# Hash attention with a token mixer: hash directions packed on the host and split in three operations, engine durations and delays of the order model read from the trace, and the order set anew

## The chip, the cores and the metric

The kernel runs on one core of a Trainium2 chip. The metric is the device time of one execution in microseconds; lower is better. The engines are TensorE (PE, with its weight loads as PEld), VectorE (DVE), ScalarE (ACT), GpSimd (POOL) and SyncE (SP), which issues the DMAs here.

## The reference

Two stages follow each other, for 4 batches, 8 heads, 768 tokens and 64 features a head:

```python
q_bits = (einsum('bhsd,dk->bhsk', q, proj) > 0)      # 6 hash bits of a query, k likewise
mask = q_bucket[:, :, :, None] == k_bucket[:, :, None, :]
scores = where(mask, q @ k.T / sqrt(D), -1e9)
attn = exp(scores - max(scores)); attn = attn / (sum(attn) + 1e-9)
x = (attn @ v), heads side by side                    # 4 x 768 x 512
theta = x @ w_theta
y = w_tok_r @ (x * cos(theta)) + w_tok_i @ (x * sin(theta))   # over the tokens
u = x + y
out = u + max(u @ w_ch, 0)
```

## The kernel before

All matrices of one batch stay on the chip. Heads go in pairs (16 pairs). The names below are those of the rows that the text shows.

**Attention.** `prep_qk` loads the transposed queries and keys of a pair (`nat`), splits each into a rounded part and its remainder (`hl`: the rounding on ACT, the subtraction, "split", on DVE or POOL), and multiplies by the hash directions (`pb`, the direction matmuls; `pst` holds the directions, positive and negated, in a rounded and a remainder part). The signs of `pb` become extra rows of the operands `qt`, `kt`, so that scores of another bucket come out hugely negative. `maxima` computes the scores once for the row maxima (`sq`, nine DVE maxima `mc` a head), transposes them (`pmx`) and puts the row back by DMA. `step` computes the scores again with the keys on the partitions (`st`), in nine chunks of 512 a head; ACT takes the exponential (`pf`). Then comes the product with the values (`po`) in one of two forms:

- the two-part form: ACT rounds `pf` to 16 bits (`p1`), POOL takes the remainder (`p2`), and three 16-bit matmuls are made per tile of 128 keys and 128 queries (two with 65 columns, one with 64), with the values in two 16-bit parts (`vv`);
- the full form, for the pairs listed in `FULL`: one fp32 matmul with 65 columns per tile, from `pf` and fp32 values (`vw`), and no `p1`, `p2`.

DVE scales the result into the batch's tile `x` (`recip`, `norm`).

**Mixer.** `moe`: each of 6 token tiles is transposed (`pt_x`), split (`h_x`, `l_x`) and multiplied by `w_theta` (`ps_th`); DVE and ACT reduce the angle, ACT takes cosine and sine for a group of tiles at once (a table load stands ahead of each group), DVE multiplies with `x` (`f`), ACT and POOL or DVE split the product (`z`, the angles' remainder); 216 matmuls `py` mix the tokens; a second product `ps_r` by `w_ch` ends it. The weights of the tokens are unpacked from 64-bit words during the first batch (`prep_wtok`, tile `wst`: low and high word on DVE, sign and magnitude on ACT, product on POOL or DVE, split into `wtk`).

**The order.** Every piece of work is an `op` with a priority, the engines that may do it with a duration for each, the ops that it needs and the buffers that it holds. `issue_all` runs a list schedule over them at build time: an engine that is free takes the ready op of the lowest key, and the instructions are issued in the order so found. The durations and the delays between engines in it (`SAME`, `LAT` and the numbers in the op calls) decide the order alone; on the chip, an instruction starts when the one ahead of it on its engine and the semaphores that it waits for allow. Where PE has nothing to do in the model during the first 190 us, a filler matmul is issued (`fill<-idle`), which nothing uses. Priorities come from the constants at the end of the file (for example `W0`, the place of the token weights among the steps).

Of the kernel before, what the change touches and what calls it, by code (L numbers as in the profile page):

```python
# [32 lines left out]
def lsh_attention_moe_kernel(ctx: ExitStack, tc: tile.TileContext, qk, wt, v, proj, w_theta, w_ch, aff, out):  # L33
# [4 lines left out]
    NB = proj.shape[1]  # L38
    DM = w_theta.shape[0]
    P = 128  # L40
# [19 lines left out]
    affs = const.tile([P, 2], F32, name="affs")  # L60
# [10 lines left out]
    pp = const.tile([P, NB], F32, name="pp")  # L71
    pst = {}
    for nm in "qk":
        for part in "hl":
            pst[nm, part] = const.tile([P, P], F32R, name=f"pst_{nm}{part}")
            DVE.memset(pst[nm, part].bitcast(F32), 0.0)
# [6 lines left out]
    SAME = {"PE": 0, "ACT": 120, "DVE": 115, "POOL": 160}  # L83
# [30 lines left out]
    def issue_all():  # L114
# [98 lines left out]
        while todo:  # L213
            progress = False
            for e in START:
# [34 lines left out]
                lat = LAT.get(e, 0)  # L250
# [20 lines left out]
                if TRACE is not None:  # L271
                    TRACE.append((e, o.name, o.phase, now, dur))
                tick += 1
                same = [c for c in succ[o] if e != "SP" and list(c.alts) == [e]]
                o.same = same
                heapq.heappush(events, (now + dur + lat, tick, o))
                heapq.heappush(events, (now + dur, -tick, []))
                if same:
                    heapq.heappush(events, (now + dur + SAME[e], tick + 0.5, same))
                for c in succ[o]:  # L280
                    c.unissued -= 1
                    c.at = max(c.at, now + dur + (SAME[e] if c in same else lat))
# [10 lines left out]
            while events and events[0][0] <= now:  # L293
# [3 lines left out]
                else:  # L297
# [4 lines left out]
                    nexts = [c for c in succ[o] if c not in o.same]  # L302
# [31 lines left out]
    def load_consts():  # L334
        for j in range(2):
            dma(pp[j * D : (j + 1) * D, :], proj)
        dma(affs, aff)

    def split_proj():
        for nm, base, first in (("q", 0, 1.0), ("k", 32, -1.0)):  # L340
            for j in range(2):
                rows = slice(j * D, (j + 1) * D)
                for n, sgn in enumerate((first, -first)):
                    c0 = base + j * 2 * NB + n * NB
                    h_, l_ = (pst[nm, part][rows, c0 : c0 + NB] for part in "hl")
                    DVE.tensor_scalar(h_, pp[rows, :], sgn, None, ALU.mult)
                    DVE.scalar_tensor_tensor(l_, pp[rows, :], sgn, h_.bitcast(F32), ALU.mult, ALU.subtract)

    cload = op("consts", QKL + 0.03, on("SP", [(625, 0)] * 3, load_consts))
    proj_ready = op("pst", QK0, on("DVE", 2200, split_proj), [cload])  # L350


# [71 lines left out]
    def prep_wtok(n, prio):  # L424
# [22 lines left out]
        def split():  # L447
# [11 lines left out]
            "POOL": (100 + 1650, lambda: POOL.tensor_tensor(t["f"], t["f"], t["sg"], ALU.mult)),  # L459
            "DVE": (60 + 830, lambda: DVE.tensor_tensor(t["f"], t["f"], t["sg"], ALU.mult)),  # L460
        }, [d, e], sl)
        i = op("wth", prio, on("ACT", 100 + 640, lambda: ACT.activation(hi16, t["f"], AF.Copy, scale=wsc[:, col])), [g, h_], sl)
        wready["tk"].append(op("wtl", prio, on("DVE", 60 + 830, split), [i], sl))
        wst_last.append(wready["tk"][-1])

    def join_wtok(prio):
# [25 lines left out]
        o = op("vall", prio, on("DVE", 130, row), [o], [sa])  # L492
        o = op("vall", prio, on("PE", 130, everywhere), [o], [sa])
# [8 lines left out]
    def prep_v(b, hp, prio):  # L502
# [104 lines left out]
        d = op("vmean", prio, on("PE", 220, mean), [c], [svb, sm_])  # L607
        e = op("vclr", prio, on("POOL", 600, clear), [r], [sv])
# [623 lines left out]
```

## Time and profile before

| | |
|---|---|
| median of 3 runs | 859.31 us (858.04 to 859.6) |
| the profiled execution, its time | 857.55 us |
| its span, first to last instruction | 855.7 us |
| mean granted TensorE clock | 0.99 |
| PE busy | 819.1 us, of which filler matmuls 53.1 us (131) |
| DVE, ACT, POOL busy | 554.3, 514.9, 471.2 us |

Busy is the time in which an engine has an instruction in flight; PE's matmuls overlap, so a busy PE is not one at its peak. A row of the timeline gives start and length in us, engine, line, operation, tiles written and read, shapes, a count of merged instructions, and in brackets the idle time before and who ended it. The group rows give busy time and mean ns, then the idle time before them. The stages are the start (0 to 80 us), the rest of the first batch's attention (to some 220 us), then three times the attention of a batch beside the mixer of the batch before it, and the mixer of batch 3 alone (from some 760 us).

### The profile page before, as it was taken

What the parts mean: (1) busy time and instruction counts of PE and PEld (TensorE: products, weight loads), DVE (VectorE), ACT (ScalarE), POOL (GpSimd) and SP (SyncE); (2) the same over time, 40 slices, a digit from 0 to 9 for tenths busy, and PEclk for the clock granted to TensorE, in tenths of its full rate; (3) what the DMA queues carried; (4) which work ended last, traced back from release to release, by engine and by line L of the source; (5) the groups of instructions that cost most, each with busy time, mean ns of one, the idle gap of its engine ahead of it and who ended that gap; (6) DMA issues with size and microseconds to landing.
All of it is one profiled execution on the core that took longest, in us unless ns stands there. A gap on an engine that the chain in (4) does not pass through costs nothing.

```text
span 855.7 us, 17506 instructions
## 1 busy us (share of the span) xinstructions
PE 819.1 (96%) x6726; PEld 575.0 (67%) x6726; DVE 554.3 (65%) x957; ACT 514.9 (60%) x881; POOL 471.2 (55%) x503
## 2 busy tenths in 40 slices
PE   8998999999999999997999999999999999999997
PEld 3477678768666577765766767778667766676455
DVE  5876879985897755766788555565796445138123
ACT  3264877786984635684897545557987453559000
POOL 3332875685786525794569645576669463653100
PEclk9996999999999999999999999999999999999999
DMA  7375576534433332544331524334342412000001
GB/s 222 80 194 156 109 209 199 165 76 108 99 87 79 115 81 72 137 100 94 81 88 33 130 68 109 73 91 109 78 96 59 103 25 65 13 15 1 1 12 62
DMA packets 33779, 78.99 MB, mean 92 GB/s; under 512 B 6520, under 2 KB 10808, under 8 KB 33696
## 3 DMA queue, kind: packets, MB, share of 16 engines
q1 hardware_dynamic: 33696, 77.88, 36.4%
q8 instruction: 53, 0.87, 0.4%
q14 instruction: 30, 0.25, 0.1%
HBM read 32.51 MB, written 6.29 MB: 45 GB/s over the span
## 4 chain that ended last, share of the span: by engine, by line
PE 81%; DVE 7%; ACT 6%; issue 2%; POOL 2%; DMA 1%; SPq 0%; POOLq 0%; ACTq 0%; DVEq 0%
PE py L79 20%; PE st L79 13%; PE po L79 13%; PE ps_r L79 8%; PE ps_th L79 7%; PE sq L79 6%; PE fill L79 5%; PE pb L79 4%; DVE mc L767 2%; ACT pf L845 2%; PE pt_u L956 1%; DVE hl L645 1%; DVE mc L776 1%; ACT p L851 1%; PE pt_x L956 1%
## 5 line engine op out<-in xcount | busy, mean ns | idle before, releaser
L857 POOL TENSOR_TENSOR p<-pf,p 128x512 f16<-128x512 f32 x252 | 301.4, 1219 | 135.4 <-ACT p L851 87.8
L845 ACT ACTIVATE pf<-st 128x512 f32<-128x512 f32 x288 | 166.4, 593 | 123.9 <-PE st L79 99.4
L767 DVE TENSOR_REDUCE mc<-sq 128x1 f32<-128x512 f32 (+1 forms) x288 | 190.3, 683 | 63.1 <-PE sq L79 61.4
L79 PE MATMUL py<-z,wtk 128*128 128x512 f16 x864 | 213.1, 380 | 0.0
L79 PE MATMUL st<-qt,kt 108*128 108x512 f32 (+3 forms) x768 | 194.8, 367 | 3.7 <-ACT pf L845 3.1
L851 ACT ACTIVATE p<-pf 128x512 f16<-128x512 f32 x252 | 152.3, 630 | 30.1 <-PE po L79 27.9
L79 PEld LDWEIGHTS st<-qt,kt 108*128 108x128 f32 (+1 forms) x768 | 120.7, 192 | 27.2 <-ACT pf L845 13.2
L79 PEld LDWEIGHTS <-p 128*128 128x128 f16 x3024 | 113.0, 98 | 35.6 <-issue 20.7
L79 PE MATMUL po<-vv,p 128*128 128x65 f16 x3024 | 131.2, 194 | 3.4 <-POOL p L857 2.5
L79 PEld LDWEIGHTS <-wtk 128*128 128x128 f16 x864 | 73.5, 98 | 83.9 <-issue 16.3
L79 PE MATMUL sq<-kt,qt 108*128 108x256 f32 (+1 forms) x384 | 123.8, 390 | 1.1 <-DVE mc L767 0.6
L79 PEld LDWEIGHTS sq<-kt,qt 108*128 108x128 f32 x384 | 67.7, 192 | 22.5 <-DVE mc L767 8.0
L1045 POOL TENSOR_TENSOR z<-f,z 128x512 f16<-128x512 f32 x35 | 49.7, 1432 | 52.4 <-ACT z L1039 52.1
L79 PE MATMUL ps_r<-wch,h_u 128*128 128x512 f32 x192 | 62.4, 406 | 0.7 <-ACT h_u L961 0.7
L79 PE MATMUL ps_th<-wth,h_x 128*128 128x512 f32 x192 | 62.2, 405 | 0.9 <-ACT h_x L961 0.9
L79 PE MATMUL fill<-idle 128*128 128x512 f16 x131 | 53.1, 409 | 6.0 <-DVE idle L68 1.6
L961 ACT ACTIVATE h_u<-pt_u 128x512 fp32r<-128x512 f32 x24 | 14.2, 595 | 73.9 <-PE pt_u L956 73.9
L1080 DVE SCALAR_TENSOR_TENSOR x<-ps_r,x 128x512 f32<-128x512 f32 x24 | 16.6, 691 | 60.0 <-PE ps_r L79 60.0
L1034 DVE SCALAR_TENSOR_TENSOR f<-x,zr,z 128x512 f32<-128x512 f32 x48 | 50.1, 1079 | 4.5 <-POOL z L1045 2.1
L788 POOL TENSOR_SCALAR fl<-row 6x128 f16<-6x128 f32 x32 | 23.3, 729 | 38.9 <-DVE row L784 24.6
L79 PE MATMUL po<-vw,pf 128*128 128x65 f32 x288 | 39.1, 287 | 4.7 <-ACT pf L845 4.6
L552 POOL TENSOR_TENSOR vb<-vb 128x384 f32<-128x384 f32 x16 | 16.1, 1009 | 48.3 <-DVE vv L549 23.3
(146 smaller groups left out, 1110.5 us busy)
## 6 DMA issues: line engine op xcount, KB each, us to landing
nat<-in_qk_dram SPq DMA_DIRECT2D x32, 384.0 KB
qt<-hl SPq DMA_DIRECT2D x31, 384.0 KB
kt<-hl SPq DMA_DIRECT2D x31, 384.0 KB
wst<-in_wt_dram SPq DMA_DIRECT2D x12, 768.0 KB
vb<-in_v_dram SPq DMA_DIRECT2D x16, 384.0 KB
out_dram<-x SPq DMA_DIRECT2D x24, 256.0 KB
qt<-hl SPq DMA_DIRECT2D x62, 96.0 KB
kt<-hl SPq DMA_DIRECT2D x62, 96.0 KB
```

Source lines behind the costliest of these rows:

```text
L79: PE.matmul(out_, l, r, start=start, stop=stop, skip_group_check=True)
L552: POOL.tensor_tensor(t["vb"][:, :, 0:3], t["vb"][:, :, 0:3], t["vb"][:, :, 3:6], ALU.add)
L767: DVE.tensor_reduce(col()[:, cs], u["sq"], AX.X, ALU.max)
L788: POOL.tensor_scalar(t["fl"], t["row"].bitcast(F32), -BIG / 4, PSC, ALU.is_lt, ALU.mult)
L845: ACT.activation(wide("pf", spf, F32), u["st"], AF.Exp, scale=1.0 / math.sqrt(D))
L851: ACT.activation(o_, u["pf"], AF.Copy)
L857: return lambda: eng.tensor_tensor(wide("p2", sp2, F16), u["pf"], u["p1"], ALU.subtract)
L956: PE.transpose(u["pt"][:, c], src()[:, c * P : (c + 1) * P], ident)
L961: ACT.activation(u["hi"], u["pt"], AF.Copy)
L1034: DVE.scalar_tensor_tensor(u["f"], tl[b][:, tt], t["zr"][:, 2 * tt + r : 2 * tt + r + 1], t["zw"][r][:, tt], ALU.mult, ALU.mult)
L1045: return lambda: eng.tensor_tensor(t["z"][r, 1][:, tt], u["f"], t["z"][r, 0][:, tt], ALU.subtract)
L1080: DVE.scalar_tensor_tensor(tl[b][:, to], r_["ps"], 0.0, tl[b][:, to], ALU.max, ALU.add)
```

## The change

Three parts. First, the host packs signs, thresholds and directions into one array, so that one DMA replaces three, and three DVE operations over both halves replace sixteen small ones; POOL clears the target in one operation where DVE cleared it in four. The stationary operand of the direction matmuls has 64 columns instead of 128.

```diff
-    pp = const.tile([P, NB], F32, name="pp")
+    pjs = const.tile([P, 2, 2 * NM], F32, name="pjs")
+    psts = const.tile([P, 2, 2, 96], F32R, name="pst")
+    POOL.memset(psts.bitcast(F32), 0.0)
...
     def load_consts():
-        for j in range(2):
-            dma(pp[j * D : (j + 1) * D, :], proj)
-        dma(affs, aff)
+        dma(cst, consts)
 
     def split_proj():
-        for nm, base, first in (("q", 0, 1.0), ("k", 32, -1.0)):
...
-                    DVE.tensor_scalar(h_, pp[rows, :], sgn, None, ALU.mult)
-                    DVE.scalar_tensor_tensor(l_, pp[rows, :], sgn, h_.bitcast(F32), ALU.mult, ALU.subtract)
+        h_, l_ = psts[:, 0, :, : 2 * NM], psts[:, 1, :, : 2 * NM]
+        DVE.tensor_tensor(pjs, sgns.rearrange("p (i n) -> p i n", i=2), pj.unsqueeze(1).to_broadcast([P, 2, 2 * NM]), ALU.mult)
+        DVE.tensor_copy(h_, pjs)
+        DVE.tensor_tensor(l_, pjs, h_.bitcast(F32), ALU.subtract)
...
-                            mm(u["pb"][:, :n_], pst[nm, a_], t["hl"][:, c, i, lo : lo + n_], n == 0, n == 5)
+                            mm(u["pb"][:64, :n_], pst[nm, a_], t["hl"][:, c, i, lo : lo + n_], n == 0, n == 5)
```

Second, the model that sets the order gets other numbers: a delay for the end of an operation by engine (and for some by name), one for the waking of each engine, an extra one for the weights' preparation, and other durations.

```diff
-    LAT = {"PE": 220, "ACT": 120, "DVE": 115, "POOL": 140}
+    TAIL_ = {"PE": 165, "ACT": 112, "DVE": 84, "POOL": 52, "SP": 0}
+    TAILS = {"st": 240, "qmax": 240, "pv": 200, "bits": 245, "vall": 100, "vmean": 70, "pv4": 245}
+    LAZY = dict.fromkeys(("wlow", "whigh", "wsign", "wabs", "wscale", "wmul", "wth", "wtl", "wh", "wl"), 200)
+    WAKE = {"ACT": 45, "DVE": 37, "PE": 58, "POOL": 105, "SP": 40}
...
-        f = op("flag", pr, on("POOL", 220, flag), [r], [smc])
+        f = op("flag", pr, on("POOL", 690, flag), [r], [smc])
```

Third, the constants of the order are others throughout; three of them change what is computed where: a third pair in the full form, remainders on POOL or DVE, and the angles of batches 0 to 2 in three groups of two tiles instead of two groups of three.

```diff
-FULL = [0, 2]
+FULL = [0, 1, 2]
...
-P1 = [[0, 999, ['ACT']]]
-P2 = [[0, 999, ['POOL']]]
-GR = 0
+P1 = [[0, 12, ['ACT', 'DVE']], [12, 999, ['ACT']]]
+P2 = [[0, 999, ['POOL', 'DVE']]]
+GR = 2
...
-W0 = 5.196
+W0 = 2.347
```

Counted over the whole order: fillers 131 before and 121 now; remainders 252 on POOL before, 135 on POOL and 99 on DVE now; splits of queries and keys 17 on DVE and 15 on POOL before, 8 and 24 now; activation tables loaded 14 times before, 20 now.

The start, on DVE. Before, the first split, the first of the sixteen direction operations, the last of them and what follows:

```order
L76 MEMSET pst_kl 128x128
L645 TENSOR_TENSOR hl_0_153<-nat_0_0_130,hl_0_153 128x768
L346 TENSOR_SCALAR pst_qh<-pp 64x6
L347 SCALAR_TENSOR_TENSOR pst_ql<-pp,pst_qh 64x6
...
L347 SCALAR_TENSOR_TENSOR pst_kl<-pp,pst_kh 64x6
L517 TENSOR_REDUCE vam_0_205<-vb_0_149 128x1
L694 CAST kt_120<-hl_0_153 64x1536
```

Now, at the same place:

```order
L72 MEMSET ones_92 1x2
L348 TENSOR_TENSOR pjs<-cst 128x48
L349 CAST pst<-pjs 128x2x24
L350 TENSOR_TENSOR pst<-pjs,pst 128x2x24
L646 TENSOR_TENSOR hl_0_149<-nat_0_0_124,hl_0_149 128x768
L646 TENSOR_TENSOR hl_0_149<-nat_0_0_131,hl_0_149 128x768
L519 TENSOR_REDUCE vam_0_171<-vb_0_135 128x1
L695 CAST kt_114<-hl_0_149 64x1536
```

The direction operations stand ahead of the splits now, and both splits of the first pair are DVE's, where the second was POOL's. On PE 18 fillers stood ahead of the first direction matmul, now 13; ahead of the first attention output 73, now 60.

The second head of batch 0, on ACT (L845, now L846, is the exponential; L454 and L455 are sign and magnitude of a token weight; `wf_th`, `wth` belong to `w_theta`). Before:

```order
L845 ACTIVATE pf_1_0_0_671<-st_1_0_0_633 128x512
L454 ACTIVATE wst_606<-wst_606 128x768
L455 ACTIVATE wst_606,wam<-wst_606 128x768
L454 ACTIVATE wst_621<-wst_621 128x768
L845 ACTIVATE pf_1_0_1_715<-st_1_0_1_700 128x512
L455 ACTIVATE wst_621,wam<-wst_621 128x768
L462 ACTIVATE wtk_105<-wst_606,wsc 128x768
L845 ACTIVATE pf_1_0_2_732<-st_1_0_2_718 128x512
```

Now:

```order
L846 ACTIVATE pf_1_0_0_630<-st_1_0_0_620 128x512
L846 ACTIVATE pf_1_0_1_638<-st_1_0_1_627 128x512
L846 ACTIVATE pf_1_0_2_653<-st_1_0_2_640 128x512
L846 ACTIVATE pf_1_1_0_663<-st_1_1_0_648 128x512
L393 ACTIVATE wf_th_0_542<-wf_th_0_542 128x512
L643 ACTIVATE hl_2_707<-nat_0_2_393 128x768
L846 ACTIVATE pf_1_0_3_715<-st_1_0_3_659 128x512
```

The two token weights stand no longer between the first exponentials of this head; the next two now stand ahead of and among those of the head after it.

The end of batch 1's attention, on DVE, where head 1 of batch 2 has its maxima (`mc_1`). Before:

```order
L767 TENSOR_REDUCE mc_1_5415<-sq_1_6_5510 128x1
L767 TENSOR_REDUCE mc_1_5415<-sq_1_7_5531 128x1
L645 TENSOR_TENSOR hl_1_5446<-nat_2_1_5134,hl_1_5446 128x768
L767 TENSOR_REDUCE mc_1_5415<-sq_1_8_5550 128x2
L900 RECIPROCAL rc_7_1_5589<-po_7_0_5331 128x6
L776 TENSOR_TENSOR mc_1_5415<-mc_1_5415 128x6
L906 SCALAR_TENSOR_TENSOR x_3180<-po_7_0_5331,vinv,rc_7_1_5589 128x6x64
```

Now (L858 is a remainder):

```order
L768 TENSOR_REDUCE mc_1_5204<-sq_1_5_5278 128x2
L858 TENSOR_TENSOR p_2_0_0_0_5300<-pf_0_0_0_5267,p_2_0_0_0_5276 128x512
L768 TENSOR_REDUCE mc_1_5204<-sq_1_6_5296 128x1
L768 TENSOR_REDUCE mc_1_5204<-sq_1_7_5302 128x1
L901 RECIPROCAL rc_7_1_5356<-po_7_0_5057 128x6
L907 SCALAR_TENSOR_TENSOR x_2789<-po_7_0_5057,vinv,rc_7_1_5356 128x6x64
L858 TENSOR_TENSOR p_2_0_0_3_5363<-pf_0_0_3_5304,p_2_0_0_3_5345 128x512
```

The split of the next pair has left DVE for POOL, and single remainders stand between the maxima and behind the scaling of the attention output.

More of the change, by code (lines that the diff above doesn't have):

```diff
@@ L32, in lsh_attention_moe_kernel @@
 @with_exitstack
-def lsh_attention_moe_kernel(ctx: ExitStack, tc: tile.TileContext, qk, wt, v, proj, w_theta, w_ch, aff, out):
+def lsh_attention_moe_kernel(ctx: ExitStack, tc: tile.TileContext, qk, wt, v, consts, w_theta, w_ch, out):
     nc = tc.nc
@@ L70, in lsh_attention_moe_kernel @@
     DVE.memset(ones1, 1.0)
-    pp = const.tile([P, NB], F32, name="pp")
+    pjs = const.tile([P, 2, 2 * NM], F32, name="pjs")
+    psts = const.tile([P, 2, 2, 96], F32R, name="pst")
+    POOL.memset(psts.bitcast(F32), 0.0)
     pst = {}
[L73 to L76, printed above, removed]
+    for i, part in enumerate("hl"):
+        flat = psts[:, i].rearrange("p a b -> p (a b)")
+        pst["q", part], pst["k", part] = flat[:, :64], flat[:, 64:128]
     def mm(out_, l, r, start, stop):
@@ L301, in issue_all @@
                             free[sl.pool].append(sl.idx)
-                    nexts = [c for c in succ[o] if c not in o.same]
+                    nexts = []
                 for c in nexts:
@@ L334, in load_consts @@
     def load_consts():
-        for j in range(2):
-            dma(pp[j * D : (j + 1) * D, :], proj)
-        dma(affs, aff)
+        dma(cst, consts)
     def split_proj():
-        for nm, base, first in (("q", 0, 1.0), ("k", 32, -1.0)):
[L341 to L350, printed above, removed]
+        h_, l_ = psts[:, 0, :, : 2 * NM], psts[:, 1, :, : 2 * NM]
+        DVE.tensor_tensor(pjs, sgns.rearrange("p (i n) -> p i n", i=2), pj.unsqueeze(1).to_broadcast([P, 2, 2 * NM]), ALU.mult)
+        DVE.tensor_copy(h_, pjs)
+        DVE.tensor_tensor(l_, pjs, h_.bitcast(F32), ALU.subtract)
+    cload = op("consts", QKL + 0.005, on("SP", [(600, 0)], load_consts))
+    proj_ready = op("pst", QK0 - 0.01, on("DVE", 720, split_proj), [cload])
     wth = [wp.tile([P, NC, DM], F32R, name=f"wth{i}") for i in range(2)]
@@ L1127 @@
 SETS = 3
-CL = 0.356
+CL = 0.214
 TAIL = ["m", "s"]
@@ L1151, with _consts @@
 SEED = 162248
[L1152 to L1188 removed]
+TH0_3 = 4.023
+TH1_3 = 0.304
+Y0_3 = 16.204
+YS_3 = 7.658
+Y1_3 = 3.219
+MX0_0 = -2.545
+MX1_0 = -0.458
+AS0_0 = -5.127
+PV0_0 = -3.986
+QK0_0 = -2.659
+QK1_0 = -8.282
+HOLD = 0.312
+FILL = 190000
+TH0_0 = 0.49
+TH1_0 = 0.849
+Y0_0 = 10.381
+Y1_0 = 1.107
+YS_0 = 5.176
+AHEAD = 1.931
+QKL = -8.066
+QK0 = -3.777
+QK1 = -5.44
+AS0 = -1.124
+PV0 = -4.578
+LV0 = -3.999
+W0 = 2.347
+WS = 1.758
+TH0 = 0.512
+TH1 = 0.818
+Y0 = 10.167
+YS = 6.472
+Y1 = 2.716
+_INS = ["v", "moe_w_theta", "moe_w_ch"]
+def _consts(proj):
     import numpy as np
+    d, n = proj.shape
     tiny = np.finfo(np.float32).tiny
[L1192 removed]
+    a = np.zeros((128, 2 + 12 * n), np.float32)
     for j in range(2):
[L1194 to L1198 removed]
+        for i in range(2):
+            c = (2 * j + i) * n
+            a[c : c + n, :2] = (0, 1) if i else (tiny, 1)
+            a[32 + c : 32 + c + n, :2] = (tiny, -BIG) if i else (0, -BIG)
+            a[:, 2 + c : 2 + c + n] = -1 if i else 1
+            a[:, 2 + 4 * n + c : 2 + 4 * n + c + n] = 1 if i else -1
+            a[j * d : (j + 1) * d, 2 + 8 * n + c : 2 + 8 * n + c + n] = proj
     return a
```

159 lines of the change are left out of this document (63 added, 96 removed).

## The prediction

> **What bounds the kernel now.** I read the page first (engines, slices), then busy time by stage, then the idle filler matmuls, then the two stretches in which TensorE lost most. The page's shares, and the granted clock over 40 slices:
>
> ```profile
> PE 819.1 (96%) x6726; PEld 575.0 (67%) x6726; DVE 554.3 (65%) x957; ACT 514.9 (60%) x881; POOL 471.2 (55%) x503
> ...
> PEclk9996999999999999999999999999999999999999
> ```
>
> TensorE is busy 819.1 of 855.7 us, so the reader should ask where the other 36.6 us lie, and how much of "busy" is real work. The clock falls below nine tenths in one slice only, the fourth (64 to 86 us). Busy time by stage (columns: the stretch, its length, then busy us and instructions of PE, PEld, DVE, ACT, POOL, then clock, DMA share, GB/s), and below it the same of the filler matmuls alone:
>
> ```profile
> 0.00:80.00 80.00, 70.15 (x306) 43.24 (x307) 55.99 (x115) 34.78 (x54) 25.62 (x38) 0.92 0.60 166
> 60.00:80.00 20.00, 15.53 (x73) 13.97 (x73) 13.78 (x24) 11.20 (x19) 6.06 (x4) 0.70 0.67 177
> 0.00:220.30 220.30, 205.24 (x1528) 147.28 (x1529) 169.75 (x330) 139.99 (x236) 118.97 (x138) 0.97 0.58 152
> 220.30:760.00 539.70, 524.82 (x4767) 373.79 (x4763) 346.69 (x575) 347.59 (x605) 341.74 (x358) 1.00 0.34 81
> 340.00:400.00 60.00, 51.66 (x601) 40.33 (x600) 42.59 (x64) 40.49 (x72) 46.41 (x51) 0.97 0.51 118
> 400.00:760.00 360.00, 355.77 (x3241) 255.43 (x3240) 215.61 (x365) 233.35 (x396) 224.21 (x235) 1.00 0.32 74
> 760.00:855.70 95.70, 89.06 (x444) 53.89 (x440) 37.90 (x54) 27.28 (x41) 10.46 (x8) 1.00 0.05 20
> ```
>
> ```profile
> 0.00:80.00 80.00, 31.27 (x73) 0.92 0.60 166
> 80.00:180.00 100.00, 15.17 (x41) 0.99 0.63 165
> 180.00:226.00 46.00, 6.66 (x18) 1.00 0.38 90
> ```
>
> So TensorE bounds 400 to 760 (98.8% busy) and the tail; there is little to win there by order. The loss is in the first 220 us, where 53.1 us of "busy" is filler and DVE is the fullest of the others (169.75), and in 340 to 400, where TensorE idles 8.3 us. A new order has to win it there.
>
> **The start.** Rows of the timeline: SP, ACT, DVE and then PE (start, us, instruction).
>
> ```profile
> 0.74 0.86 SPq L637 DMA_DIRECT2D nat<-in_qk_dram  x2
> ...
> 5.07 0.84 ACT L642 ACTIVATE hl<-nat 128x768 fp32r<-128x768 f32 x1 [0.16 <-DMA nat<-in_qk_dram]
> ...
> 4.94 0.96 DVE L645 TENSOR_TENSOR hl<-nat,hl 128x768 fp32r<-128x768 f32 x1 [2.84 <-ACT hl L642]
> 5.82 0.16 DVE L346 TENSOR_SCALAR pst_qh<-pp 64x6 fp32r<-64x6 f32 x1
> 6.01 1.82 DVE L347 SCALAR_TENSOR_TENSOR pst_ql<-pp,pst_qh 64x6 fp32r<-64x6 f32 x1
> ...
> 10.00 0.16 DVE L347 SCALAR_TENSOR_TENSOR pst_kl<-pp,pst_kh 64x6 fp32r<-64x6 f32 x1
> ...
> 1.56 11.49 PE L79 MATMUL fill<-idle 128*128 128x512 f16 x18 [1.56 <-DVE idle L68]
> 12.56 1.34 PE L79 MATMUL pb<-hl,pst_qh 128*128 128x512 f32 x2
> ...
> 16.80 3.40 PE L79 MATMUL fill<-idle 128*128 128x512 f16 x8
> ...
> 48.59 0.19 PE L79 MATMUL po<-mt,ft 128*128 128x65 f16 x1
> ```
>
> The 16 direction operations hold DVE from 5.82 to 10.16, yet the first direction matmul starts at 12.56: what ends last before it is the 18 fillers, which stand ahead of it on PE's queue. After the change 13 stand there, at (12.56 - 1.56) / 18 = 0.61 us each 5 x 0.61 = **3.1 us** less, so it starts at about 9.5. Is its data there? The second input load is moved one DMA issue back on SP's queue (0.86 / 2 = 0.43), so ACT's copy starts at 5.5, DVE's split after it (0.96, now on DVE, not POOL) ends at 7.4; the three new DVE operations are bounded by the shortest and longest rows of the old ones, 0.16 and 1.82 each, and stand ahead of the splits, waiting for the packed load. I take 0.2 as nearest: ready by 7.5. Even with one at 1.82 it is 9.1. The four DVE clears (one POOL clear now) lie ahead of both and cost nothing, the loads cover them. Term: -3.1, bounds 0 and -3.1. The narrower 64-column direction weights change no streamed column, and PEld is 67% busy beside PE: 0.
>
> From the first direction matmul to the first attention output (48.59) stand 55 fillers before and 47 after. At 3.40 / 8 = 0.425 us, 8 fewer are worth 3.4 us if nothing is late behind them; DVE has 24 us free in the first 80. I take **-3**, bounds 0 and -3.4.
>
> **The hole at 63 us.** Rows of PE, ACT and DVE:
>
> ```profile
> 55.67 1.00 PE L79 MATMUL po<-vw,pf 128*128 128x65 f32 x8
> ...
> 67.85 1.97 PE L79 MATMUL po<-vw,pf 128*128 128x65 f32 x8 [4.47 <-ACT pf L845]
> 71.44 1.80 PE L79 MATMUL po<-vw,pf 128*128 128x65 f32 x8
> ...
> 66.44 0.88 ACT L454 ACTIVATE wst<-wst 128x768 f32<-128x768 f32 x1 [2.39 <-DVE wst L442]
> 67.22 0.58 ACT L845 ACTIVATE pf<-st 128x512 f32<-128x512 f32 x1
> ...
> 64.31 2.10 DVE L442 SCALAR_TENSOR_TENSOR wst<-wst 128x768 uint32<-128x768 uint32 x1
> ```
>
> The exponential that PE waits 4.47 us for stands on ACT behind the sign of a token weight, which waits for DVE's unpacking, which waited for its load. Afterwards the same 8 matmuls take 1.80 instead of 1.00; the granted clock is 0.70 over 60 to 80, which is 0.30 x 20 = 6 us of full speed. Loss: 4.5 + 6 = 10.5. In the new order four exponentials of that head stand in a row with no token weight between; the next pair of weights is unpacked a head later, and its two loads stand on SP behind six copies of a head's operands instead of ahead of them, which costs nothing as long as the unpacking stands later still. There a short wait of the same kind may come back (its sign stands ahead of head 2's first exponential). I take **-9**, bounds 0 and -10.5.
>
> **The third pair in full precision.** It takes 18 chunks from the two-part form. The groups that go, and PE's rates for both forms:
>
> ```profile
> L857 POOL TENSOR_TENSOR p<-pf,p 128x512 f16<-128x512 f32 x252 | 301.4, 1219 | 135.4 <-ACT p L851 87.8
> ...
> L851 ACT ACTIVATE p<-pf 128x512 f16<-128x512 f32 x252 | 152.3, 630 | 30.1 <-PE po L79 27.9
> ...
> 49.46 2.20 PE L79 MATMUL po<-vw,pf 128*128 128x65 f32 x18
> ...
> 683.20 1.55 PE po L79 x50
> ```
>
> POOL loses 18 x 1.219 = 21.9 us and ACT 18 x 0.630 = 11.3, all in the first 220 us, where neither is the fullest. PE gives 72 x 2.20 / 18 = 8.8 us for 216 x 1.55 / 50 = 6.7, so +2.1; the 15.2 us of fillers at 80 to 180 cover it, and if they are needed elsewhere it costs 2.1. I take **+1**, bounds 0 and +2.1.
>
> **The hole at 390 us.** Rows of DVE, POOL and PE, and the spread of that DVE operation:
>
> ```profile
> 387.93 6.81 DVE L645 TENSOR_TENSOR hl<-nat,hl 128x768 fp32r<-128x768 f32 x1
> ...
> 386.04 7.88 POOL L857 TENSOR_TENSOR p<-pf,p 128x512 f16<-128x512 f32 x7
> ...
> 396.15 0.47 PE L956 MATMUL pt_x<-ident,x 128*128 128x128 f32 x1 [5.46 <-DVE x L906]
> ...
> L645 DVE TENSOR_TENSOR hl<-nat,hl x17: 939/1048/6809, 4.9 to 667.6; 128x768 fp32r<-128x768 f32 x17
> ```
>
> A DVE split of 0.94 us lasts 6.81, until POOL's run of seven remainders ends; the attention output that PE's transposes need is queued behind it on DVE. At 400 to 760's idle share (1.2%) the 60 us would idle 0.7 instead of 8.3, so 7.6 is at stake. In the new order both splits of that pair are POOL's, and its run there is cut by remainders given to DVE. I take **-6**, bounds 0 and -7.6.
>
> **Remainders on DVE.** By the new order 99 of 234 go there, 91 of them behind the first angle product, so after some 220 us. No such row exists; the nearest is the remainder of the angles, the same tile, types and operation:
>
> ```profile
> L1045 DVE TENSOR_TENSOR z<-f,z x13: 691/1233/2327, 222.9 to 795.0; 128x512 f16<-128x512 f32 x13
> ...
> L1022 ACT ACT_TABLE_LOAD  x7: 1283/1283/1283, 216.0 to 771.8; - x7
> ```
>
> At the median 91 x 1.23 = 112 us come to DVE's 346.7 from 220 to 760, and 7 of the 9 splits that now go to POOL (7 x 1.05) leave it here: 452 of some 530, 85%. DVE does not bound the stage, but the angle stretches are full already, and DVE's scaling of outputs queues behind a remainder. Between 0 (all hidden) and the 5.9 us of one starved split, I take **+3**, by the median row.
>
> The Trainium skill's page "SBUF — State Buffer" says in its section "Who interferes with whom" that a DVE operation with two SBUF inputs and a POOL one that reads SBUF exclude each other, and that whoever issues first keeps the shared port for its whole instruction. If that were all, a remainder on DVE would wait for one POOL remainder at most, 0.69 + 1.22, and 91 of them would bring DVE to some 514 us of the stage: still not the bound, and a starved split would not exist. The row of 6.81 under a run of seven disagrees with "one at most", so the sum goes by the row.
>
> **The rest.** Angles in three groups of two tokens instead of two of three: 6 more table loads, 6 x 1.283 = 7.7 us on ACT, which is 64% busy there; the first group starts a token earlier. Bounds -3 and +7.7; nearest to hidden, **+1**. In the tail PE idles 6.6 us of 95.7, and leftover projections now stand between the last angles: **-1**, bounds -3 and +3. Two multiplications of token weights go from DVE to POOL, and the maxima of batch 0 run from the last block to the first; all nine are needed before anything follows, and POOL is half idle in the first 220 us: 0. The rest of the reordering lies where PE is 98.8% busy: 0.
>
> Sum: -3.1 - 3 - 9 + 1 - 6 + 3 + 1 - 1 = -17.1. The profiled execution took 857.55, so 840.5; the median of the runs shown, 859.31, is 1.8 above it: **842**.
>
> **Rivals.** About 0.2% (1.7 us) is what a measurement of this kernel can tell from no change.
> - *The waits come back elsewhere*: the new order puts other weights and splits ahead of what PE waits for, and half of the two holes' 15 returns. 842 + 8 = 850. For it: head 2's exponentials stand behind a token weight.
> - *Starved DVE* (the other side): remainders or splits on DVE wait out POOL runs, as at 387.93, in the attention-only stretches of batches 1 to 3, with DVE's outputs behind them. Each costs 7.6. With three, the terms of 390 us and of the remainders (-6 + 3) give way to +22.8: 868; with two, 860, no change. It decides from three on. Against it: POOL's remainders fall from 252 to 135, so long runs are rarer.
> - *Everything is hidden*: fillers shrink and the waits stand where they were, no change.
> - *All ends are the good ones*: -3.1 - 3.4 - 10.5 - 7.6 - 3 = -27.6: 832; with the angles' -3, 829.
>
> **How the numbers follow.** Forecast 0.57, waits come back 0.20, good ends 0.08: faster 0.85. No change 0.05 (hidden, or two starved). Slower 0.10. The range takes the low end of all bounds and, above, 850 plus one starved split: 828 to 858.
>
> **What would show it.** Right: the first direction matmul near 9.5 us and the first attention output near 42; no slice with a clock under 0.9 after the start; PE idle in the middle of the run under 2%; DVE remainders near 1.2 us on average. Wrong: a DVE operation of several microseconds beside a POOL run, PE idle after it; or DVE over 90% busy for 40 us on end with PE waiting for its maxima.

## The result, and the profile after

The changed kernel takes 829.18 us (median of 4 runs, 827.61 to 830.03) where the kernel before took 858.67 on the same chip: a ratio of 0.9656, 95% interval 0.9635 to 0.9677, faster by 29.5 us. The forecast was 842 with a range of 828 to 858: the sign held, the centre was 13 us too high, and the range held by 1.2 us only (one of the four runs, 827.61, lies below it). The profiled execution took 830.03 us, its span 828.2; the spans of the two profiles differ by 27.5 us. Of the runs below, one of e2_thin (988.78 us) and one of e5_pool (864.03 us) were in a slow state with a lower clock and are left out of the medians and ratios.

The page of the changed kernel, the lines that answer to those of before:

```profile
PE 808.8 (98%) x6644; PEld 569.7 (69%) x6644; DVE 602.8 (73%) x1024; ACT 511.1 (62%) x871; POOL 372.9 (45%) x404
...
PEclk9999999999999999999999999999999999999999
```

TensorE's idle time fell from 36.6 to 19.4 us, its busy time from 819.1 to 808.8, and the slice with a lowered clock is gone. Load moved from POOL (471.2 to 372.9) to DVE (554.3 to 602.8). Busy time by stage, now (the last attention ends some 27 us earlier, so its stage is taken to 740), and the fillers alone:

```profile
0.00:80.00 80.00, 76.04 (x421) 50.88 (x421) 59.06 (x115) 39.92 (x63) 30.07 (x42) 1.00 0.64 176
60.00:80.00 20.00, 20.00 (x151) 17.97 (x150) 17.86 (x32) 13.14 (x23) 10.48 (x7) 1.00 0.71 196
80.00:220.30 140.30, 135.08 (x1117) 105.14 (x1115) 118.91 (x222) 101.98 (x173) 73.34 (x81) 1.00 0.54 142
220.30:340.00 119.70, 119.60 (x996) 80.58 (x996) 91.99 (x147) 73.24 (x137) 66.33 (x69) 1.00 0.37 97
340.00:400.00 60.00, 58.29 (x597) 44.63 (x597) 49.89 (x88) 49.88 (x88) 38.28 (x45) 1.00 0.53 119
400.00:740.00 340.00, 337.19 (x3135) 238.91 (x3135) 247.59 (x410) 219.16 (x374) 156.14 (x163) 1.00 0.31 73
740.00:828.20 88.20, 82.61 (x388) 49.60 (x387) 35.39 (x46) 26.91 (x40) 8.78 (x7) 1.00 0.05 18
```

```profile
0.00:80.00 80.00, 28.50 (x69) 1.00 0.64 176
80.00:220.30 140.30, 19.53 (x52) 1.00 0.54 142
```

Two stretches of before that the prediction did not show by themselves:

```profile
80.00:220.30 140.30, 135.09 (x1224) 104.03 (x1223) 113.76 (x215) 105.20 (x182) 93.36 (x100) 0.99 0.57 144
220.30:340.00 119.70, 117.38 (x928) 78.03 (x924) 88.48 (x146) 73.75 (x137) 71.12 (x73) 1.00 0.32 83
```

From these rows, stretch by stretch, the change of TensorE's idle time (length less busy), of the fillers (53.10 - 31.27 = 21.83 in the second stretch before), and of the clock. The clock's loss is summed from windows of one microsecond, (1 - granted clock) each: before, 6.8 us at 67 to 82 and 1.7 at 395 to 399; after, none.

| stretch | forecast | idle | fillers | clock | third pair | found |
|---|---|---|---|---|---|---|
| 0 to 80 | -15.1 | -5.9 | -2.8 | -6.1 | | -14.8 |
| 80 to 220 | +1 | 0.0 | -2.3 | -0.8 | +2.1 | -1.0 |
| 220 to 340 and 400 to the tail | +4 | -2.2 - 1.4 | | | | -3.6 |
| 340 to 400 | -6 | -6.6 | | -1.7 | | -8.3 |
| the tail | -1 | -1.05 | | | | -1.05 |

The third pair is taken as the prediction works it out, not measured. The column found sums to -28.7, 1.2 more than the spans differ by, in part because idle time under the lowered clock is counted twice. The clock terms are those of one execution of the kernel before: with the order at these places untouched, e1_pack's profile lost 8.5 and 3.4 us there instead of 6.8 and 1.7. So in sum the first 80 us came out as forecast, and the miss lies behind: mostly in the stretches where remainders on DVE and more table loads were to cost 4 us and where 3.6 were won.

What TensorE waited for (its largest rows; total us, times, longest), before and then after:

```profile
PE pt_x L956 <- DVE x L906: 5.5, 1, 5.5
PE po L79 <- ACT pf L845: 4.6, 2, 4.5
PE st L79 <- ACT pf L845: 3.1, 7, 0.8
PE po L79 <- POOL p L857: 2.5, 5, 0.8
```

```profile
PE st L82 <- ACT pf L846: 2.6, 5, 0.8
...
PE po L82 <- DVE p L858: 0.4, 1, 0.4
```

Both holes are gone, and so is the wait for POOL's remainders.

### The profile page after: what moved, and what is told of

Its sections match the earlier page's. It is cut to its first block, busy times and chain, and to the rows that moved or that the text cites. A ratio compares the mean times of both kernels' runs of the same rounds, so it can differ in the third digit from the quotient of the medians.

```text
span 828.2 us, 17207 instructions
## 1 busy us (share of the span) xinstructions
PE 808.8 (98%) x6644; PEld 569.7 (69%) x6644; DVE 602.8 (73%) x1024; ACT 511.1 (62%) x871; POOL 372.9 (45%) x404
## 4 chain that ended last, share of the span: by engine, by line
PE 87%; DVE 6%; ACT 4%; issue 1%; DMA 1%; SPq 1%; ACTq 0%; DVEq 0%
PE py L82 21%; PE po L82 15%; PE st L82 15%; PE ps_r L82 8%; PE sq L82 8%; PE ps_th L82 7%; PE fill L82 5%; PE pb L82 4%; DVE mc L768 2%; PE pt_u L957 1%; PE pt_x L957 1%; ACT pf L846 1%; PE pa L82 1%; ACT p L852 1%; DVE mc L777 1%
## 5 line engine op out<-in xcount | busy, mean ns | idle before, releaser
L846 ACT ACTIVATE pf<-st 128x512 f32<-128x512 f32 x288 | 167.8, 596 | 134.2 <-PE st L82 126.3
L858 POOL TENSOR_TENSOR p<-pf,p 128x512 f16<-128x512 f32 x135 | 167.5, 1252 | 182.7 <-ACT p L852 119.8
L852 ACT ACTIVATE p<-pf 128x512 f16<-128x512 f32 x234 | 140.7, 632 | 9.2 <-PE po L82 7.0
L82 PE MATMUL sq<-kt,qt 108*128 108x512 f32 (+1 forms) x384 | 128.9, 393 | 2.7 <-DVE mc L768 1.2
L82 PEld LDWEIGHTS <-p 128*128 128x128 f16 x2808 | 106.8, 98 | 31.1 <-issue 14.0
L82 PE MATMUL po<-vv,p 128*128 128x65 f16 (+1 forms) x2808 | 124.5, 193 | 0.4 <-DVE p L858 0.4
L858 DVE TENSOR_TENSOR p<-pf,p 128x512 f16<-128x512 f32 x99 | 87.5, 888 | 35.0 <-ACT p L852 32.9
L82 PEld LDWEIGHTS po<-vw,pf 128*128 128x128 f32 x432 | 54.5, 192 | 1.8 <-issue 0.2
L82 PE MATMUL po<-vw,pf 128*128 128x65 f32 x432 | 54.6, 274 | 0.0
L82 PE MATMUL fill<-idle 128*128 128x512 f16 x121 | 48.0, 404 | 5.5 <-DVE ones L72 1.6
L646 POOL TENSOR_TENSOR hl<-nat,hl 128x768 fp32r<-128x768 f32 x24 | 48.1, 2013 | 10.6 <-ACT hl L643 10.5
```

What stands on the lines that cost most here:

```text
L82: PE.matmul(out_, l, r, start=start, stop=stop, skip_group_check=True)
L646: return lambda: eng.tensor_tensor(t["hl"][:, 1, i], u["nat"], t["hl"][:, 0, i].bitcast(F32), ALU.subtract)
L846: ACT.activation(wide("pf", spf, F32), u["st"], AF.Exp, scale=1.0 / math.sqrt(D))
L852: ACT.activation(o_, u["pf"], AF.Copy)
L858: return lambda: eng.tensor_tensor(wide("p2", sp2, F16), u["pf"], u["p1"], ALU.subtract)
```

## The experiments

Ten of the twelve kernels keep an order and change one thing or a few in it; two, e6_model and e8_full2, have their order set anew. The ratios are to runs of the kernel before on the same chip (medians 858.1 to 858.8).

| kernel | edit | median, us | ratio, 95% interval | lost to the clock, us |
|---|---|---|---|---|
| before | | 858.7 | 1 | 8.5 |
| e1_pack | directions packed | 857.86 | 0.9988 (0.9970 to 1.0006) | 11.9 |
| e2_thin | and 5 fillers fewer | 856.38 | 0.9972 (0.9961 to 0.9983) | 11.9 |
| e3_split | starved split to POOL | 858.70 | 1.0002 (0.9993 to 1.0011) | 11.9 |
| e4_weight | one weight later on ACT | 857.55 | 0.9986 (0.9978 to 0.9995) | 10.2 |
| f1_chain | one weight later on ACT, DVE, POOL | 854.79 | 0.9958 (0.9944 to 0.9971) | 10.2 |
| f2_run | POOL's run broken | 854.63 | 0.9961 (0.9948 to 0.9973) | 8.5 |
| f3_all | e2, f1 and f2 together | 847.49 | 0.9881 (0.9867 to 0.9894) | 10.2 |
| g1_later | four weights and their loads later | 859.45 | 1.0011 (1.0003 to 1.0020) | 8.5 |
| g3_light | and 18 remainders left out | 855.28 | 0.9977 (0.9959 to 0.9995) | 6.8 |
| e6_model | new model alone, order anew | 880.61 | 1.0281 (1.0244 to 1.0318) | 23.8 |
| e5_pool | after, no remainder on DVE | 841.97 | 0.9813 (0.9800 to 0.9827) | 0 |
| e8_full2 | after, two full pairs, order anew | 847.57 | 0.9879 (0.9860 to 0.9898) | 22.1 |
| after | | 829.18 | 0.9656 (0.9635 to 0.9677) | 0 |

The last column is summed from the profiled execution as above, without the last microseconds, in which TensorE has ended. It varies with no edit near the place: the fall at the hole at 63 us cost 6.8 us in the profile of before and 8.5 in that of e3_split, whose one moved instruction stands at 388 us; the fall at 390 us cost 1.7 in before and 3.4 in e4_weight, whose edit is at 66 us. The runs of before beside the experiments had a mean clock of 0.985 to 0.988, which is a loss of 10 to 13 us.

### The start: e1_pack and e2_thin

e1_pack takes the first part of the change alone; the places and counts of all else stay, 18 fillers too. e2_thin leaves out the last 5 of those:

```diff
+        fillers.append(0)
+        skip = 13 < len(fillers) <= 18
-        return op("fill", 0, on("PE", 225, lambda: mm(bank(sl, [P, 512], "fill"), ...)))
+        return op("fill", 0, on("PE", 225, lambda: skip or mm(bank(sl, [P, 512], "fill"), ...)))
```

> The kernel before with the first part of the change alone: packed directions, one load for three, three direction operations for sixteen; every engine's order else kept, so 18 fillers still stand ahead of the first direction matmul. Theory (the fillers end last there): the first direction matmul stays at 12.5 us and the time does not move, 0 within 1.7 us. Rival (the sixteen operations and the loads set the pace): the matmul starts 1 to 2 us earlier and the time falls by as much.

> The same as the kernel with packed directions alone, with the last 5 of the 18 fillers ahead of the first direction matmul left out and nothing else moved. Theory: the first direction matmul starts at 9.5 us and the end comes 3.1 us earlier than with packing alone (855.6 where before took 858.7). Rival: something after the start (the maxima on DVE, the loads) is late anyway and takes the 3 us back: no change.

With 18 fillers the first direction matmul of e1_pack began at 12.56 us as before, and the time did not move (the interval holds 1): the theory. The direction matmuls of e1_pack, then the start and the hole of e2_thin (PE's timeline; start, length, operation, in brackets the idle time ahead and what ended it):

```profile
12.56 2.82 PE L82 MATMUL pb<-hl,pst 128*64 128x512 f32 x12
```

```profile
1.55 8.29 PE L82 MATMUL fill<-idle 128*128 128x512 f16 x13 [1.55 <-DVE ones L72]
9.36 4.06 PE L82 MATMUL pb<-hl,pst 128*64 128x512 f32 x12
...
66.39 1.97 PE L82 MATMUL po<-vw,pf 128*128 128x65 f32 x8 [6.43 <-ACT pf L843]
```

The fillers end last at the start, as both theories' first halves said: with 5 fewer the first direction matmul comes 3.2 us earlier. The time falls by 2.4 us against before (interval 1.5 to 3.3) and by 1.5 against e1_pack (857.86 to 856.38). So the theory's 3.1 is within the interval, the rival's "no change" is not, and how much of the step is lost behind the start can't be told. The transposed maxima of the first two heads come at 31.5 and 48.5 us, 1.9 us earlier than in e1_pack and 3.4 earlier than in before.

Then TensorE waits at the hole for 6.43 us, longer than the 4.47 in the profile of before. The edit need not be the reason: in e1_pack, e3_split and f2_run, whose order at the hole is that of before, this wait took 5.67, 6.18 and 6.07 us.

### The hole at 63 us: e4_weight, f1_chain, g1_later, g3_light

e4_weight holds back one weight's sign and magnitude on ACT for two exponentials; f1_chain holds back the whole chain from the unpacking on for four (first and second part; what depends on a held operation is held with it):

```diff
+        if o.name == "wsign" and count["wsign"] == 5:
+            held.append((o, fn))
...
+        if token and seen_["wst"] == 4:
+            held.append((o, fn))
```

> The kernel before with ACT's order changed at one place: the sign and magnitude of the token weight at 66.44 us stand behind the next two exponentials instead of ahead of and between them. Theory: the exponential at 67.22 us comes at 64.1, TensorE's wait of 4.47 us shrinks to 1.4, the granted clock at 60 to 80 us rises from 0.70 to over 0.9, and the time falls by 3 us for the wait and up to 6 for the clock: 6 to 9, to some 850 to 853. Rival: the clock falls for another reason, or the weights' chain that follows is late instead: the time falls by 3 us at most.

In e4_weight the exponential came 3.4 us earlier and TensorE waited 1.21 us for it, but next it waited for DVE's maxima, behind an unpacking that waited for its load (PE, then DVE):

```profile
69.10 1.39 PE L79 MATMUL sq<-kt,qt 108*128 108x256 f32 x3 [3.58 <-DVE mc L792]
...
65.83 0.56 DVE L464 TENSOR_SCALAR wst<-wst 128x768 uint32<-128x768 uint32 x1 [3.75 <-DMA wst<-in_wt_dram]
```

> The kernel before with the whole chain of one token weight (unpacking on DVE, sign and magnitude on ACT, product on POOL) behind the fourth exponential after it, so that nothing which waits for that weight's load stands ahead of head 1's exponentials and head 2's maxima. The reordering of ACT alone only handed TensorE's wait from ACT's exponential (4.47 us) to DVE's maxima (3.58 us), behind an unpacking that waited for the load. Theory (the load is what ends last, through DVE and ACT): both waits go, the granted clock at 60 to 80 us is over 0.9, and the time falls by 6 to 10 us, to 849 to 853. Rival (the weight is needed there, or other transfers are late too): a wait of 3 us or more stays between 60 and 75 us and the time falls by 2 us at most.

With the chain out of DVE's way too, waits of 1.20 and 2.42 us stayed, the second behind ACT's rounding of the next pair, which waited for a transfer (the row names the last one issued; the tile that ACT writes, `hl`, is also read by the six copies ahead of it). PE, ACT, and the stretch:

```profile
71.94 1.22 PE L79 MATMUL st<-qt,kt 108*128 108x256 f32 x4 [2.42 <-ACT pf L871]
...
70.56 0.84 ACT L668 ACTIVATE hl<-nat 128x768 fp32r<-128x768 f32 x1 [4.02 <-DMA w_th<-in_moe_w_theta_dram]
...
60.00:70.00 10.00, 8.02 (x46) 6.36 (x45) 7.72 (x15) 3.71 (x6) 2.31 (x2) 0.83 0.97 191
```

The time fell by 3.3 us, between theory and rival. The DMA engines were busy 97% of these ten us. In SP's queue of before two loads of weights stand ahead of the copies of a head's operands. After the change the copies come first:

```profile
53.47 0.34 SPq L433 DMA_DIRECT2D wst<-in_wt_dram  x1
...
55.51 0.38 SPq L433 DMA_DIRECT2D wst<-in_wt_dram  x1
...
57.63 1.46 SPq L716 DMA_DIRECT2D qt<-hl  x1
```

```profile
49.10 0.70 SPq L717 DMA_DIRECT2D qt<-hl  x1
...
54.36 1.38 SPq L721 DMA_DIRECT2D kt<-hl  x1
...
56.47 0.90 SPq L435 DMA_DIRECT2D wst<-in_wt_dram  x2
```

That the load is the last link shows in profiles with the same order at the hole: DVE's unpacking waited 0.84, 2.75, 3.59 and 3.63 us for the load of the second of these two weights (before, e1_pack, f2_run, e3_split), and TensorE's wait was 4.47, 5.67, 6.07 and 6.18.

g1_later makes this move on the order of before, and more with it: the loads of the third and fourth weight go behind the copies, and everything that unpacks the third to sixth comes nine exponentials later (the loads of the fifth and sixth too).

```diff
+        if any(sl in weights[2:6] for sl in mine):
+            held.append((count["pf"] + (4 if token and len(weights) <= 4 else 9), fn, o))
+            return
```

> The kernel before with the third to sixth token weight later in the order of every queue: the loads of the third and fourth behind the six copies of a head's operands on SP (they stood ahead of them), and everything that unpacks them nine exponentials later, so two heads of maxima stand ahead. With the unpacking alone moved back (loads not), the wait went on to ACT's rounding of the next pair, 4.02 us behind copies that shared the wires with two loads of weights. Theory (at 63 us the transfers are late, because the loads of weights are issued ahead of the copies that the next head waits for): no wait of TensorE over 1.5 us at 55 to 80, the granted clock there over 0.9, and the time falls by 8 to 11 us, to 847 to 850. Rival (the loads only move the hole to where they are issued now): a wait of 3 us or more at 65 to 100, and the time falls by 4 us at most.

The hole closed, as the theory had it, with the clock at 1.00. As loads and unpacking moved together, this does not show what the place of the loads does by itself. And all of the gain was given back in the next 50 us. g1_later's stretches, its next waits on PE, and the transposed maxima of heads 3 to 6 (first and last start) in before and in g1_later:

```profile
60.00:80.00 20.00, 19.16 (x137) 17.01 (x136) 13.21 (x25) 9.47 (x17) 3.94 (x4) 1.00 0.76 221
80.00:100.00 20.00, 15.87 (x91) 10.35 (x90) 16.90 (x30) 13.41 (x25) 14.31 (x17) 0.76 0.50 130
...
83.15 0.51 PE L79 MATMUL sq<-kt,qt 108*128 108x256 f32 x2 [1.29 <-DVE mc L790]
```

```profile
L780 PE MATMUL pmx<-ident,mc x4: 269/272/415, 80.8 to 128.7; 128*6 128x128 f32 x4
```

```profile
L803 PE MATMUL pmx<-ident,mc x4: 269/272/273, 70.9 to 130.4; 128*6 128x128 f32 x4
```

9.9 us ahead at the third head, 1.7 behind at the sixth. g3_light asked whether POOL's remainders of the second pair take it back; its products use the rounded exponentials in their place.

```diff
+                    if g < 4 * NQ and not vt["full"]:
+                        return lambda: u.update(p2=u["p1"])
```

> The kernel before with the later token weights of the run above (which has no hole at 63 us, is 9.3 us ahead at the end of the third head's maxima, and has lost all of it by 129 us), and with POOL's 18 remainders of the second pair left out: its products take the rounded exponentials twice, so this part of the values is not computed. Order else kept. Theory (between 80 and 129 us the remainders of the second pair, on POOL, take the gain back; the third full pair of the change removes just these): the gain stays, the fifth head's maxima end 8 us or more earlier than before, and the time is 849 to 852. Rival (ACT, DVE and the falls of the clock take it back, with POOL or without): the time stays within 3 us of the run without this edit, 856 to 861.

Only in part: the sixth head's maxima came 3.5 us earlier than in g1_later (at 126.9 us), the end 4.2 us. Some 8 of the 11.6 us are taken back without them. The row at 83 us names DVE's maxima (so does the next wait, at 85 us), and the clock fell again from 83 to 91 us; that the weights' unpacking, now at that place, makes these maxima late is likely from DVE's order but was not tried by itself. The time, 855.28, lies between the two, 0.7 us under the rival's range: nearer the rival on the sum, with the theory right on a third of it.

### The hole at 390 us: e3_split and f2_run

```diff
+                        e_ = POOL if eng is DVE and len(splits) == 9 else eng            # e3_split
+                        e_ = DVE if len(rest) in (109, 111, 113) else eng                # f2_run
```

> The kernel before with one instruction moved: the split of queries that took 6.81 us on DVE at 387.93 us is POOL's. Theory: the hole of 5.46 us on TensorE at 390 us closes, and the time falls by 6 us (bounds 0 and 7.6), to some 852.7. Rival: the split then stands in POOL's run of remainders, and the direction matmuls and remainders behind it are late instead: the time falls by 2 us or less.

The time did not move (858.70). The hole stayed at 4.07 us, and 1.39 us were added ahead of it by a remainder that stood behind the moved split on POOL, as the rival had it: 5.46, as before. With the split gone, the next operation with two operands in SBUF took its place on DVE, 6.53 us for what takes 0.15 when alone (e3_split: PE, DVE, POOL):

```profile
396.82 0.47 PE L962 MATMUL pt_x<-ident,x 128*128 128x128 f32 x1 [4.07 <-DVE x L912]
...
389.71 6.53 DVE L782 TENSOR_TENSOR mc<-mc 128x6 f32<-128x6 f32 x1
...
390.60 5.62 POOL L863 TENSOR_TENSOR p<-pf,p 128x512 f16<-128x512 f32 x5
```

> The kernel before with three of the seven remainders of POOL's run at 386 to 394 us given to DVE, order kept. Moving the starved split alone handed the starvation to the next DVE operation with two operands in SBUF (6.53 us for one of 0.16). Theory (it is the run without a gap that starves DVE, whatever stands there): no DVE operation over 2.5 us at 380 to 400, TensorE's wait of 5.46 us for x falls under 2, and the time falls by 4 to 6 us, to 853 to 855. Rival (x is late for another reason): the wait stays above 4 us and the time falls by 1 us at most.

With three of the run's seven remainders on DVE, the split ended with the shorter run, the wait for x was gone, and TensorE's longest wait there was 1.99 us (f2_run: PE, DVE, POOL). The time fell by 3.5 us, a little less than the 4 to 6 expected: another wait of 2 us stands there now, for one of the remainders given to DVE.

```profile
392.42 0.24 PE L79 MATMUL po<-vv,p 128*128 128x65 f16 x1 [1.99 <-DVE p L860]
...
388.41 2.39 DVE L645 TENSOR_TENSOR hl<-nat,hl 128x768 fp32r<-128x768 f32 x1
...
386.58 3.40 POOL L860 TENSOR_TENSOR p<-pf,p 128x512 f16<-128x512 f32 x3
```

So the run makes these waits, and not what stands on DVE.

### The parts together: f3_all

Its edits are those of e2_thin, f1_chain and f2_run.

> The kernel before with four edits together, order else kept: packed directions, 13 fillers ahead of the first direction matmul, the token weight's chain moved back, the run of remainders broken. Theory (the terms are independent once the hole at 63 us no longer takes the start's gain back): 3.1 + 6 to 10 + 4 to 6, in all 13 to 19 us: 840 to 846. Rival (a further wait takes a gain back, as the hole at 63 us did with 2.7 of the start's 3.4): 849 or more.

847.49 lies between theory and rival: -10.6 us where the three alone gave -2.4, -3.3 and -3.5. They add up within their intervals (that the hole takes 2.7 of the start's 3.4, as the rival has it, compares two profiles only); but some third of what was expected did not come, and the clock still fell at 61 to 76 us (6.8 us), here after a wait of only 1.15 us. So the repairs, put into the order of before, give 10.6 of the 29.5 us. The other 19 come with the new order as a whole, and apart from e5_pool no run takes them apart.

### Remainders on DVE: e5_pool

```diff
-                k2 = op("p2", G + KB, pick(g, P2, {"DVE": (600, p2(DVE)), "POOL": (1116, p2(POOL))}), ...)
+                k2 = op("p2", G + KB, pick(g, P2, {"DVE": (600, p2(POOL)), "POOL": (1116, p2(POOL))}), ...)
```

> The changed kernel, its order kept, with the 99 remainders that DVE takes given to POOL. By the prediction's term (remainders on DVE cost 3 us) this would be 3 us faster than the changed kernel: 826. Theory now (they cost nothing on DVE, and on POOL they make runs that starve DVE and make the products wait, POOL's load rising from 373 us by 99 x 1.24 = 123): slower by 5 us or more, with DVE operations of over 4 us again: 834 to 845.

12.8 us slower than the changed kernel (841.97 against 829.18; 13.5 by the two ratios). The size is the theory's, its way only in part: no DVE operation is starved for over 2.7 us. What grows are the waits for POOL's remainders, on PE, on its weight loads and on ACT, whose buffers come free later. e5_pool, then the changed kernel:

```profile
PE po L82 <- POOL p L858: 6.9, 14, 0.9
...
ACT pf L846 <- POOL p L858: 16.3, 21, 2.2
...
PEld L82 <- POOL p L858: 9.5, 18, 1.1
```

```profile
ACT pf L846 <- POOL p L858: 2.4, 5, 1.0
```

This is the price on an order that was set with 99 of them on DVE. What an order set for POOL alone would lose was not tried.

### The model and the third pair: e6_model and e8_full2

Both change one part and set the order anew, so that every place moves.

> The kernel before with the second part of the change alone: the new durations and delays of the order model; constants, directions and everything else as before, the order set anew from them. Theory (the gain is the order that the new constants set, the places of weights and loads and the remainders on DVE): within 6 us of before, 852 to 864. Rival (the truer model itself sets the better order): faster by 10 us or more, 848 or less.

Slower by 22 us, outside both. The new durations with the old constants make a worse order, with 23.8 us lost to the clock in six falls. So the model alone does not bring the gain; the new constants with the old model were not tried.

```diff
-FULL = [0, 1, 2]
+FULL = [0, 2]
```

> The changed kernel with two pairs in the full form instead of three (the second pair of heads goes back to the two-part form), the order set anew. By the prediction's term (a third full pair costs 1 us, bounds 0 and 2.1) this would be 827 to 829. Rival (it pays: it takes 21.9 us from POOL and 11.3 from ACT, and remainders and exponentials of the first 220 us then wait less): 832 or more, with TensorE's loss at 80 to 180 us larger.

18.4 us slower than the changed kernel, the rival's side. But its span is 849.2, 21.0 above the changed kernel's, and the falls of its clock cost 22.1 us, none in the changed kernel. e8_full2's stretches and a wait ahead of one fall:

```profile
60.00:80.00 20.00, 18.25 (x106) 16.56 (x106) 14.10 (x26) 9.76 (x16) 8.88 (x6) 0.75 0.61 179
140.00:160.00 20.00, 19.59 (x90) 16.75 (x89) 16.52 (x33) 12.17 (x21) 9.54 (x7) 0.62 0.52 180
...
69.80 0.74 PE L82 MATMUL sq<-kt,qt 108*128 108x512 f32 x1 [1.47 <-DVE winv L362]
```

With the clock's loss taken off, the profiled execution would be 1.1 us faster than the changed kernel's. But the five executions, taken so by their mean clock, give spans of 824 to 833 us beside 826 to 828, which is too wide to test a term of 1 us, and every other place in the order moved too. Its longest waits at 80 to 180 us are for DVE's maxima (1.82 and 3.05 us at 134 and 168 us), not for the exponentials or remainders that the rival names. What the third pair is worth stays open, as does whether another order with two full pairs keeps the clock up.

## Why the prediction was right, and where it was wrong

**The start** (forecast -3.1, first direction matmul at 9.5): right, 9.36, with 13 fillers ahead; the data were there, the last split ending at 7.62 against a forecast of 7.5. The changed kernel on PE and DVE:

```profile
9.36 4.11 PE L82 MATMUL pb<-hl,pst 128*64 128x512 f32 x12
...
39.55 0.19 PE L82 MATMUL po<-mt,ft 128*128 128x65 f16 x1
...
6.66 0.96 DVE L646 TENSOR_TENSOR hl<-nat,hl 128x768 fp32r<-128x768 f32 x1 [0.21 <-ACT hl L643]
```

From there to the first attention output 30.2 us pass where 36.0 did: -5.8 instead of -3, the output at 39.55, not 42. Idle time and fillers up to it fell by 7.4 us (36.2 to 28.8) where 6.1 were forecast.

**The hole at 63 us** (forecast -9): the hole closed, no wait and a clock of 1.00 at 60 to 80. From the first attention output to 80 us, idle time (4.7) and the clock (6.1) gained 10.8 us, of which 9 more fillers took 3.4 back: 7.4. With the 7.4 of the start this is the 14.8 found for the first 80 us, so that the sum met the forecast of 15.1 is in part luck: one term was too small, the other too large.

The chain of the prediction was right to its last link, the load, but it took the cure to be the order on ACT and said of the loads' new place behind six copies only that it "costs nothing". e4_weight and f1_chain show that moving the sign and the unpacking hands most of the wait on; g1_later, with loads and unpacking later, closes the hole. That the loads' place does it is likely from the waits for the load, but no run has it alone. Nor is the gain kept by itself: the rival "the waits come back elsewhere" is what happened on the old order in g1_later. It did not happen in the changed kernel; that this is because the work behind was set anew as well is argued, not shown. The forecast rested on a sum of separate terms: f3_all bears this out for three repairs, g1_later does not for this hole.

**The third pair** (forecast +1): open, since e8_full2 can't tell 1 us from none.

**The hole at 390 us** (forecast -6): 6.6 of idle time and 1.7 of clock went, -8.3; the clock, left out of this term, is most of the difference. That POOL's run starves DVE was right, and e3_split and f2_run show it. The Trainium skill's page "SBUF — State Buffer", section "Who interferes with whom", lets the engine that issues first keep the shared port for one whole instruction, by which a DVE operation with two SBUF inputs would wait for one POOL instruction at most. 6.81 us beside a run of seven, 6.53 beside five and 2.39 beside three disagree: each of the three operations ended with POOL's run or up to 0.9 us behind it.

**Remainders on DVE** (forecast +3) is the step that failed, in sign. Its groups of DVE and of POOL in the changed kernel (count, busy and mean ns of one, idle time ahead):

```profile
L858 DVE TENSOR_TENSOR p<-pf,p 128x512 f16<-128x512 f32 x99 | 87.5, 888 | 35.0 <-ACT p L852 32.9 <-POOL p L858 1.2 <-issue 0.6
...
L858 POOL TENSOR_TENSOR p<-pf,p 128x512 f16<-128x512 f32 x135 | 167.5, 1252 | 182.7 <-ACT p L852 119.8 <-issue 19.0 <-PE st L82 18.8
```

One takes 0.89 us on average on DVE and 0.69 in the median, not the median of 1.23 that the term took from the angles' remainder (1.25 on average on POOL), and DVE was busy 389 of 520 us from 220 to 740, 75%, not 85. But the price was the smaller error. The term counted only what DVE pays and not what products and exponentials no longer wait for: some 13 us by e5_pool, on the changed kernel's order. Against the kernel before the gain can't have been that large, as TensorE idled only 6.6 us there in these stretches (220 to 340, and 400 to 760), of which 3.6 went. The trace of before had shown a part of it, an ACT that waited 13.6 us for buffers that POOL held:

```profile
ACT pf L845 <- POOL p L857: 13.6, 17, 2.4
```

The prediction read "TensorE is 98.8% busy" there as "little to win".

**The rest**: for the 6 more table loads (+1) no wait stands among TensorE's largest, and the stretches with them lost idle time, so 0 is nearer. The tail (-1) came out at -1.05. "The rest of the reordering: 0" holds 1 to 2 us in the first 220.

The rival "all ends are the good ones" gave 829 to 832 and so the time, but by other terms: the start and the middle went beyond its ends, while of its -10.5 at 63 us the stretch kept 7.4, as worked out above.

## What to carry to other kernels

Follow a wait back to its last link, here a transfer and, as it seems, its place in the queue that issues it; moving the instructions between passed most of the wait on. Take a wait from more than one profile: with the same order, the one at 63 us was 4.5 to 6.2 us long. Before adding up gains of separate holes, ask what will be late next at each: on the order of before the repairs alone kept between nothing (g1_later, e3_split) and two thirds (f2_run, 3.5 of 5.5 us) of what they closed. And in a stage where the busiest engine shows 98%, look at who waits for the helper engines: sharing one helper's work between two engines was worth some 13 us there, on the changed kernel's order.

## What the runs showed of the hardware

The clock after a wait. In the kernel before it fell to a half after the wait of 4.47 us and stayed there for 13.6 us, although TensorE was busy without a gap (stretches of before):

```profile
68.00:80.00 12.00, 12.00 (x47) 11.03 (x48) 6.72 (x13) 7.31 (x12) 3.32 (x2) 0.50 0.45 152
...
82.00:84.00 2.00, 2.00 (x17) 1.86 (x16) 1.97 (x5) 0.16 (x1) 0.28 (x1) 1.00 0.01 2
```

In all kernels here the loss of a fall is near a multiple of 1.7 us (1.7, 3.4, 5.1, 6.8, 8.5, 10.2), that is of 3.4 us at half the clock. The length of the wait does not set it: in one execution of before 4.47 us cost 6.8 and 5.46 cost 1.7; a wait of 1.47 us was followed by a loss of 6.8 in e8_full2 and by none in e5_pool. Nor does the order alone: of e1_pack's eleven executions one took 850.82 us at a mean clock of 0.992, the others 856.7 to 859.4 at 0.985 to 0.988. The Trainium skill's page "TensorE: Matmul & The Clock Gate", section "Part 1: The HAM clock gate", says that about 3.4 us of sustained activity release the clock; the step of 3.4 us agrees with these numbers, the 12 busy us at 0.50 do not. In that stretch TensorE ran fp32 products of 65 columns between score matmuls, and the clock came back some 3 us after the direction matmuls of 512 columns had begun; in a busy share both look alike. That the kind of matmul decides this was not tried.

The first microseconds. In every profile TensorE runs at first at half the rate of later, though the profile's clock stands at 1.00 there: direction matmuls of 512 columns follow each other at 0.43 us, then at some 0.22. The change came between some 10 and 17 us, and not at the same time with the same order at the start: the twelve direction matmuls that begin at 12.56 us had ended at 16.85 in before and at 15.61 in e3_split. So a gain or loss of 1 us behind the start can't be read from one profile of each kernel. The prediction's two prices of a filler, 0.61 and 0.425 us, lie on the two sides of this change.
